# An attention and mixing kernel on one Trainium2 core: the first batches' attention issued younger pair first, with conversions, transfers, and strided work moved around it

## The chip, the cores and the metric

The kernel runs on one core of one Trainium2 chip. The engines are PE (matrix products), DVE (vector work), ACT (activations and copies), POOL (GpSimd), and SP, which here issues most DMAs. The metric is device time in microseconds of one execution. Each engine works through its own instructions in order; an instruction waits for those on other engines whose results it needs.

## The reference

Eight batches, eight heads, 576 positions, 64 elements per head. Heads 0 to 3 attend to a window of 32 positions, heads 4 to 7 to the earlier positions of the same class modulo 32. The result x (576 x 512 for each batch) goes through a low-rank mixing along the sequence (rank 32) and a two-layer network.

```
scores = scale * np.matmul(q, k.transpose(0, 1, 3, 2))
mask_local = (rel >= 0) & (rel < stride)
mask_strided = (rel >= 0) & (pos[None, :] % stride == pos[:, None] % stride)
...
attn = np.exp(scores)
attn = attn / (np.sum(attn, axis=-1, keepdims=True) + 1e-09)
return np.matmul(attn, v).astype(np.float32)
...
h = xt @ U @ V
u = x + h.transpose(0, 2, 1)
ch = np.maximum(u @ w_ch1, 0.0) @ w_ch2
return (u + ch).astype(np.float32)
```

The inner width of the network is 2048.

## The kernel before

**Precision.** fp32 products are made of three products of split operands: high by high, low by high, high by low (uh, ul for u; gh, gl for relu's output; two parts for each weight). U, V and the weights arrive as 64-bit words and are converted on the chip by `to_f32`: L127 on ACT, L129 and L130 on DVE; for a weight L203 (ACT) then makes the high part and L204 (DVE) the low part. U's and V's copies and parts are L142 to L154.

**Units of weights.** A unit is half or all of one of 16 slices fc of the inner width: w0a is the W1 half of fc 0, w0b its W2 half; from fc 7 on one unit holds both. `load_weights` issues their DMAs ahead of time, some held by a 1x1 copy on POOL (L167), a gate; `weights` converts them.

**The first attention.** Batches 0 and 1 go through `first_attention`. A pair is two heads; the eight pairs in `heads` are batch 0's pairs 2, 3, 0, 1 and then batch 1's (numbered 0 to 7 here). Each is a generator: load of q and k, load of v, scores (masks by L338, products by L344), softmax (maximum L354 and subtraction L355 on DVE, exponential L359 on ACT), transposition (L366 on PE, copy L369 on ACT), outputs (L379), normalisation (L388 to L395 on DVE). For batch 0 a fourth step `quarter` follows: transposition of x (L310), its product with U (L284, L286), copies tst (L289, L290 on ACT, L291 on DVE), the product with V (L293) onto the transposed x, and uh (L298, ACT) and ul (L299, DVE). A loop over ticks steps all pairs that are under way, oldest first. `small_weights` loads and converts U and V between. PSUM has two tiles `acc` and one `px` of two banks each; `psx2` hands them out in turn in this part (two of three times acc).

**The main loop.** For each group of 512 tokens and each fc: `gemm1` (12 products, L649), relu to gh (L653, ACT) and gl (L654, DVE), and, one step behind, `gemm2` (12 products, L666). Two slots belong to each fc; at each slot `advance` steps the next batch's attention and mixing (`mix_t` L511 to L526, `mix_u` L534 and L536, `mix_tail` L543 to L549, `transposes` L620, `split`), and `strided_upto` the strided heads of batches 2 to 7: one transfer st, then POOL's products tmp (L440) and DVE's sums of them (L442), later L468 and L470. S0 and S1 give the slots at which it begins and ends; batch 2's first transfer is held by a copy on POOL (L425) that reads a converted weight.

**What sets the order.** A scheduler orders what is emitted by a timeline that it simulates; `issue_after(x)` makes it put an instruction behind x, with no semaphore. `marks` holds instructions for that: "less" the subtractions, "exp", "PT" the copies L369, "norm".

Of the kernel before, what the change touches and what calls it, by code (L numbers as in the profile page):

```python
# [17 lines left out]
NSP = 2  # L18
# [11 lines left out]
S0 = {2: 20, **{b: 32 * (b - 1) - 12 for b in range(3, 8)}}  # L30
S1 = (14, 14)
ORDER0 = (2, 3, 0, 1)
WARM = {0: (320,) * 3, 1: (320,) * 9 + (32,) * 6}
# [4 lines left out]
def fused_kernel(ctx, tc, pairs, strided, U, V, w_in, masks, eye, out):  # L38
# [74 lines left out]
    mask_s = early[:, 1600:1760].bitcast(BF16)  # L113
    raws, w_parts = {}, {}
# [19 lines left out]
    def small_weights():  # L134
# [5 lines left out]
        with tc.issue_after(marks["PT"][0]):  # L140
            f = to_f32(words_in, early, 128, 10 * R)
        nc.scalar.copy(out=U_sb.rearrange("p t r -> p (t r)"), in_=f[:, 0:5 * R])  # L142
        nc.scalar.copy(out=late[0][:, 1816:1816 + 5 * R], in_=f[:, 5 * R:10 * R])
        with tc.issue_after(marks["PT"][0]):
            f = to_f32(words_in[0:R, 10 * R:10 * R + S], att([128, 640], "cu"), R, S)
# [3 lines left out]
        yield  # L149
# [36 lines left out]
    def weights():  # L186
        for i, (fc, x) in enumerate(units):
# [3 lines left out]
            if i < N_HALF:  # L191
                behind = marks["less"][min(7, i + 2)], marks["PT"][min(7, i + 1)]
# [78 lines left out]
    def quarter(pr):  # L271
# [26 lines left out]
        nc.scalar.copy(out=hi, in_=src)  # L298
        nc.vector.tensor_tensor(out=lo, in0=src, in1=hi.bitcast(F32), op=ALU.subtract)  # L299
# [30 lines left out]
    def scores(kT, qT, mask):  # L330
# [3 lines left out]
        with tc.issue_after(done[-1]) if len(done) == 1 else nullcontext():  # L334
            for n in WARM.get(len(done), ()):
                nc.tensor.matmul(sp[:, 0, 0:n], ident_b, mask[:, 0:n], start=True, stop=True, skip_group_check=True)
# [83 lines left out]
    def strided_heads(b):  # L420
# [3 lines left out]
        if b == NSP:  # L424
            nc.gpsimd.tensor_copy(out=st[0:1, 0:1], in_=word_of[units.index((11, None))])  # L425
# [75 lines left out]
    def mix_t(b, half):  # L501
# [8 lines left out]
        for j in range(4):  # L510
            nc.tensor.matmul(ps_a[32 * j:32 * j + 32, :], U_sb[:, j, :], xg[:, j, cs], start=True, stop=False,  # L511
                             skip_group_check=True, tile_position=(0, 32 * j))
# [54 lines left out]
    def first_attention():  # L567
# [6 lines left out]
        dma(out=mask_s, in_=masks[:, 448:768])  # L574
        dma(out=masks_sb, in_=masks[:, 0:448])
        for k, pair in enumerate(heads[0:4]):
            next(pair)
            next(pair)
            if k == 0:
                dma(out=ident, in_=eye)  # L580
            if k == 1:
                next(sw)
        load_ahead(2)
        for tick in range(len(heads) + 3):
            for k in range(len(heads)):
# [5 lines left out]
            if tick in (1, 2):  # L591
                next(sw)
# [65 lines left out]
    def gemm2(n, fc, gh, gl):  # L658
        if fc == 0:
            accs[n] = [ps_acc.tile([128, 2, 512], F32, name="acc") for _ in range(2)]  # L660
        for s in range(4):
# [3 lines left out]
            for i, (gt, part) in enumerate(((gh, 0), (gh, 1), (gl, 0))):  # L665
                nc.tensor.matmul(accs[n][s // 2][:, s % 2, :], gt[:, cs], w_parts[fc, 1][:, part, :],  # L666
                                 start=(fc == 0 and i == 0 and n > 0), stop=(fc == NFC - 1 and i == 2))
# [25 lines left out]
    def strided_upto(slot):  # L693

        nonlocal sgen, sb, sdone, s0, s1
        if sb < B and sgen is None and slot >= S0[sb]:
            sgen, sdone, s0 = strided_heads(sb), 0, slot
# [129 lines left out]
```

## Time and profile before

| | |
|---|---|
| median of 3 runs | 929.31 us (928.73 to 929.73) |
| profiled execution | 927.69 us, span 925.9 us |
| mean granted clock | 0.993 |
| PE | busy 901.9 us (97% of the span) |
| DVE | busy 549.7 us (59%) |
| ACT | busy 243.2 us (26%) |
| POOL | busy 335.5 us (36%) |

The busy times are of the whole span. PE is busy nearly throughout, and the parts where it isn't lie in the first 140 us and the last 126. The rows that follow in the text come from the views of the trace by stretches, by waits, in order of time, by groups of one shape, and from the page's list of DMA issues.

### The profile page before, as it was taken

The page shows a single profiled execution, that of the slowest core. Times are in us where ns is not written, and L with a number is a line of the kernel's source. Part 1 is how long each engine was busy: PE and PEld are TensorE (multiplying, and loading weights), DVE is VectorE, ACT ScalarE, POOL GpSimd, SP SyncE. Part 2 cuts the span into 40 slices and gives each one's busy share as a digit, 9 for nine tenths or more (in the row PEclk, how much of TensorE's full clock was granted, in tenths as well). Part 3 has the DMA queues.
Part 4 walks back from the last instruction along what each step waited for, and adds up shares of the span by engine and source line. Part 5 has one row for each costly group of instructions (what it writes and reads, how often), then busy time and mean ns, then how long its engine had stood idle before and what let it go on. Part 6 is the DMA issues. An engine that isn't in the chain of part 4 may idle for free.

```text
span 925.9 us, 16818 instructions
## 1 busy us (share of the span) xinstructions
PE 901.9 (97%) x7000; PEld 719.1 (78%) x7000; DVE 549.7 (59%) x894; ACT 243.2 (26%) x478; POOL 335.5 (36%) x375
## 2 busy tenths in 40 slices
PE   6899989999999999999999999999999999999997
PEld 4667767877887788778877787778877888888885
DVE  4569898765786587658766786667763341122111
ACT  4447522142123312241224121422142111121110
POOL 1222097344744393439443763456540000000000
PEclk9899999999999999999999999999999999999999
DMA  9779223201330124011500141014200230001001
GB/s 343 272 251 382 84 60 101 73 1 52 92 128 2 52 55 178 1 52 33 181 8 16 52 168 50 1 52 148 73 1 1 57 121 16 1 1 46 0 1 46
DMA packets 39340, 75.29 MB, mean 81 GB/s; under 512 B 6464, under 2 KB 23232, under 8 KB 37344
## 3 DMA queue, kind: packets, MB, share of 16 engines
q1 hardware_dynamic: 27744, 67.13, 20.6%
q10 hardware_dynamic: 10560, 4.73, 2.1%
q0 software_dynamic: 960, 2.36, 0.8%
q8 instruction: 55, 0.90, 0.4%
q14 instruction: 21, 0.17, 0.1%
HBM read 54.14 MB, written 11.67 MB: 71 GB/s over the span
## 4 chain that ended last, share of the span: by engine, by line
PE 89%; DVE 3%; DMA 1%; issue 1%; POOL 1%; ACT 0%; SPq 0%; DVEq 0%; ACTq 0%; POOLq 0%
PE ph L649 41%; PE acc L666 41%; PE px L344 1%; PE px L379 1%; PE px L366 1%; PE px L511 1%; DMA st<-in_strided_dram 1%; PE px L534 1%; DVE cv L130 1%; DVE cv L129 0%; DVE s_st L442 0%; POOL tmp L440 0%; DVE w L204 0%; PE px L515 0%; PE px L338 0%
## 5 line engine op out<-in xcount | busy, mean ns | idle before, releaser
L654 DVE SCALAR_TENSOR_TENSOR gl<-ph,gh 128x512 fp32r<-128x512 f32 x144 | 98.8, 687 | 221.2 <-ACT gh L653 220.5
L649 PE MATMUL ph<-uh,w 128*128 128x512 f32 x648 | 214.7, 392 | 0.0
L653 ACT ACTIVATE gh<-ph 128x512 fp32r<-128x512 f32 x144 | 86.0, 598 | 471.3 <-PE ph L649 385.7
L468 POOL TENSOR_TENSOR tmp<-st,s_st 128x448 f32<-128x448 f32 (+7 forms) x162 | 137.9, 882 | 181.0 <-DVE st L470 95.8
L440 POOL TENSOR_TENSOR tmp<-st 128x576 f32<-128x576 f32 (+6 forms) x162 | 173.8, 1114 | 79.3 <-DMA st<-in_strided_dram 69.4
L666 PE MATMUL acc<-w,gh 128*128 128x512 f32 x648 | 196.9, 391 | 0.0
L470 DVE TENSOR_REDUCE st<-tmp 128x64 f32<-128x64 f32 (+8 forms) x162 | 137.6, 880 | 16.0 <-POOL tmp L468 15.0
L649 PEld LDWEIGHTS ph<-uh,w 128*128 128x128 f32 x648 | 121.2, 188 | 26.1
L666 PEld LDWEIGHTS acc<-w,gh 128*128 128x128 f32 x648 | 121.3, 188 | 25.6
L649 PE MATMUL ph<-ul,w 128*128 128x512 f32 x324 | 127.1, 392 | 0.0
L666 PE MATMUL acc<-w,gl 128*128 128x512 f32 x324 | 121.6, 391 | 3.7 <-DVE gl L654 3.7
L442 DVE TENSOR_REDUCE s_st<-tmp 128x9 f32<-128x576 f32 (+6 forms) x162 | 86.9, 562 | 20.0 <-POOL tmp L440 19.1
L666 PEld LDWEIGHTS acc<-w,gl 128*128 128x128 f32 x324 | 60.8, 188 | 18.0 <-DVE gl L654 4.9
L649 PEld LDWEIGHTS ph<-ul,w 128*128 128x128 f32 x324 | 60.8, 188 | 12.9
L485 ACT COPY xg<-st 32x256 f32<-32x256 f32 x96 | 38.8, 404 | 8.0 <-DVE st L470 6.6
L522 DVE TENSOR_TENSOR ta<-px,ta 32x256 f32<-32x256 f32 x42 | 17.6, 420 | 36.7 <-ACT ta L520 35.7
L672 DVE TENSOR_TENSOR xg<-acc,xg 128x512 f32<-128x512 f32 x36 | 23.0, 681 | 10.2 <-PE acc L666 10.2
L536 DVE TENSOR_TENSOR xg<-px,xg 128x512 f32<-128x512 f32 x28 | 18.0, 686 | 13.1 <-PE px L534 13.1
L649 PE MATMUL ph<-uh,w6a 128*128 128x512 f32 x72 | 25.5, 401 | 0.0
L649 PE MATMUL ph<-uh,w0a 128*128 128x512 f32 x72 | 23.9, 393 | 0.0
L649 PE MATMUL ph<-uh,w1a 128*128 128x512 f32 x72 | 23.8, 389 | 0.0
L666 PE MATMUL acc<-w1b,gh 128*128 128x512 f32 x72 | 23.8, 400 | 0.0
(261 smaller groups left out, 1249.3 us busy)
## 6 DMA issues: line engine op xcount, KB each, us to landing
w<-in_w_dram SPq DMA_DIRECT2D x9, 1024.0 KB, 8.5
out_dram<-xg SPq DMA_DIRECT2D x32, 256.0 KB, 2.1
v<-in_pairs_dram SPq DMA_DIRECT2D x12, 585.0 KB, 5.1
st<-in_strided_dram SPq DMA_DIRECT2D x6, 1152.0 KB, 5.6
qk<-in_pairs_dram SPq DMA_DIRECT2D x12, 576.0 KB, 5.4
late<-in_pairs_dram SPq DMA_DIRECT2D x8, 585.0 KB, 8.8
late<-in_pairs_dram SPq DMA_DIRECT2D x8, 576.0 KB, 9.8
raw<-bt SPq DMA_DIRECT2D x128, 32.0 KB, 1.9
```

The lines of the kernel that those rows point to most:

```text
L440: nc.gpsimd.tensor_tensor(out=tmp[:, 0:n], in0=sk[:, j0:j0 + n], in1=sq[:, i:i + 1].broadcast_to([128, n, D]), op=ALU.mult)
L442: late.append(lambda tmp=tmp, n=n, i=i, j0=j0: nc.vector.tensor_reduce(out=s_st[:, i, j0:j0 + n], in_=tmp[:, 0:n], axis=AX.X, op=ALU.add))
L468: nc.gpsimd.tensor_tensor(out=tv, in0=sv[:, 0:i + 1, d0:d0 + step], in1=s_st[:, i, 0:i + 1].broadcast_to([128, i + 1, step]), op=ALU.mult)
L470: late.append(lambda tv=tv, i=i, d0=d0, step=step: nc.vector.tensor_reduce(out=o_st[:, i, d0:d0 + step], in_=tv.rearrange("p j d -> p d j" ...
L485: nc.scalar.copy(out=xg[32 * i4:32 * i4 + 32, :, cs], in_=o_st[rows, i4:16:4, :])
L522: nc.vector.tensor_tensor(out=ta, in0=ps_a[32 * j:32 * j + 32, :], in1=ta, op=ALU.add)
L536: nc.vector.tensor_tensor(out=xg[:, t + s, :], in0=pv[:, s, :], in1=xg[:, t + s, :], op=ALU.add)
L649: nc.tensor.matmul(ph, w_parts[fc, 0][:, part, 128 * dc:128 * dc + 128], ut[:, dc, :], start=(dc == dcs[0] and i == 0), stop=(dc == dcs[-1 ...
L653: marks.setdefault("gh", []).append(nc.scalar.activation(out=gh, in_=ph, func=AF.Relu).ins)
L654: low = nc.vector.scalar_tensor_tensor(out=gl, in0=ph, scalar=0.0, in1=gh.bitcast(F32), op0=ALU.max, op1=ALU.subtract)
L666: nc.tensor.matmul(accs[n][s // 2][:, s % 2, :], gt[:, cs], w_parts[fc, 1][:, part, :], start=(fc == 0 and i == 0 and n > 0), stop=(fc == ...
L672: nc.vector.tensor_tensor(out=ot, in0=accs[n][s // 2][:, s % 2, :], in1=ot, op=ALU.add)
```

## The change

- The warm-up products ahead of the first two scores (L336, on the masks) become eight and eight of 128x512 on zeros, which DVE writes first into `raw`.
- The masks and the identity are loaded through POOL's queue; on SP the loads of the pairs follow one another in another order, and U and V come behind five of them.
- In a tick the first four pairs are stepped 3, 2, 1, 0.
- U's conversion is held behind the third pair's subtraction, V's also behind the second exponential; V's by-class copies come with a later step. The first four weight units are held behind normalisations and quarters (a new mark, "split") in place of subtractions and copies.
- `mix_t` of batch 1 is held behind the third and fourth `gemm2` (a new mark, "acc").
- Batch 2's strided work: gate on unit 10 in place of 11, its transfer issued at slot 16 in place of 20, and the steps behind it spread from slot 22 to the same end.

```diff
-S0 = {2: 20, **{b: 32 * (b - 1) - 12 for b in range(3, 8)}}
+S0 = {2: 16, **{b: 32 * (b - 1) - 12 for b in range(3, 8)}}
-WARM = {0: (320,) * 3, 1: (320,) * 9 + (32,) * 6}
+WARM = {0: 8, 1: 8}
...
+    zeros = raw.rearrange("p s a d x -> p (s a d x)")[:, 0:320].bitcast(BF16)
+    nc.vector.memset(zeros, 0.0)
...
-        with tc.issue_after(marks["PT"][0]):
+        with tc.issue_after(marks["PT"][0]), tc.issue_after(marks["less"][2]):
             f = to_f32(words_in, early, 128, 10 * R)
...
-        with tc.issue_after(marks["PT"][0]):
+        yield
+        with tc.issue_after(marks["exp"][1]), tc.issue_after(marks["less"][2]):
             f = to_f32(words_in[0:R, 10 * R:10 * R + S], att([128, 640], "cu"), R, S)
...
-                behind = marks["less"][min(7, i + 2)], marks["PT"][min(7, i + 1)]
+                behind = (marks["norm"][2], marks["PT"][3]) if i == 0 else marks["split"][(0, 0, 2, 3)[i]] if i < 4 else \
+                    (marks["less"][min(7, i + 2)], marks["PT"][min(7, i + 1)])
...
-            for n in WARM.get(len(done), ()):
-                nc.tensor.matmul(sp[:, 0, 0:n], ident_b, mask[:, 0:n], start=True, stop=True, skip_group_check=True)
+            for n in range(WARM.get(len(done), 0)):
+                nc.tensor.matmul(sp[:, 0, :], zeros[:, 0:128], zeros[:, 128:640], start=True, stop=True, skip_group_check=True)
...
-            nc.gpsimd.tensor_copy(out=st[0:1, 0:1], in_=word_of[units.index((11, None))])
+            nc.gpsimd.tensor_copy(out=st[0:1, 0:1], in_=word_of[units.index((10, None))])
...
+        with tc.issue_after(marks["acc"][2 + half]) if b < NSP else nullcontext():
+            for j in range(4):
+                nc.tensor.matmul(ps_a[32 * j:32 * j + 32, :], U_sb[:, j, :], xg[:, j, cs], start=True, stop=False,
...
-        dma(out=mask_s, in_=masks[:, 448:768])
-        dma(out=masks_sb, in_=masks[:, 0:448])
-        for k, pair in enumerate(heads[0:4]):
-            next(pair)
-            next(pair)
-            if k == 0:
-                dma(out=ident, in_=eye)
-            if k == 1:
-                next(sw)
+        far_dma(out=mask_s, in_=masks[:, 448:768])
+        far_dma(out=masks_sb, in_=masks[:, 0:448])
+        far_dma(out=ident, in_=eye)
+        for first in (heads[0], heads[1], heads[0], heads[2], heads[1], sw, heads[3], heads[2], heads[3]):
+            next(first)
...
-            for k in range(len(heads)):
+            for k in (3, 2, 1, 0, 4, 5, 6, 7):
...
-            if tick in (1, 2):
+            if tick == 2:
+                next(sw)
                 next(sw)
...
-            sgen, sdone, s0 = strided_heads(sb), 0, slot
+            sgen, sdone, s0 = strided_heads(sb), 0, slot + 6 * (sb == NSP)
+            next(sgen)
...
-        want = N_STRIDED * (slot + 1 - s0) // max(1, s1 - s0)
+        want = (N_STRIDED - 1) * (slot + 1 - s0) // max(1, s1 - s0)
```

Three places show how the order of instructions moves. A row gives the line, the operation, what it writes and reads, and the tile's size; lines of the changed kernel stand some 2 to 5 further down (L359 becomes L363, L127 becomes L129).

ACT from its first exponential on, before: L127 are the first steps of U's and V's conversion, L142 to L147 their copies.

```order
L359 ACTIVATE late<-late 128x640
L369 COPY late<-acc 128x576
L127 ACTIVATE early<-xg 128x320
L127 ACTIVATE late<-xg 32x576
L142 COPY U_sb<-early 128x160
L143 COPY late<-early 128x160
L359 ACTIVATE late<-late 128x640
L146 CAST Vst<-late 32x576
L147 CAST Vst<-late 32x576
L369 COPY late<-acc 128x576
```

After:

```order
L363 ACTIVATE late<-late 128x640
L373 COPY late<-px 128x576
L129 ACTIVATE early<-xg 128x320
L363 ACTIVATE late<-late 128x640
L129 ACTIVATE late<-xg 32x576
L373 COPY late<-acc 128x576
L363 ACTIVATE late<-late 128x640
L144 COPY U_sb<-early 128x160
L145 COPY late<-early 128x160
L149 CAST Vst<-late 32x576
L150 CAST Vst<-late 32x576
```

The second exponential stood behind both conversions and U's copies; it now stands between U's first step and V's, and the third stands ahead of all copies of U and V.

DVE's first instructions, before: L354 and L355 are a pair's maximum and subtraction, L129 and L130 the steps of U (early) and V (late).

```order
L354 TENSOR_REDUCE mx<-acc 128x10
L355 TENSOR_TENSOR late<-acc,mx 128x2x5x64
L129 TENSOR_SCALAR early<-early 128x320
L354 TENSOR_REDUCE mx<-px 128x10
L130 SCALAR_TENSOR_TENSOR early<-xg,early 128x320
L129 TENSOR_SCALAR late<-late 32x576
L355 TENSOR_TENSOR late<-px,mx 128x2x5x64
L130 SCALAR_TENSOR_TENSOR late<-xg,late 32x576
L388 TENSOR_SCALAR rt<-acc 128x10
```

After:

```order
L358 TENSOR_REDUCE mx<-acc 128x10
L359 TENSOR_TENSOR late<-acc,mx 128x2x5x64
L358 TENSOR_REDUCE mx<-acc 128x10
L359 TENSOR_TENSOR late<-acc,mx 128x2x5x64
L358 TENSOR_REDUCE mx<-acc 128x10
L359 TENSOR_TENSOR late<-acc,mx 128x2x5x64
L131 TENSOR_SCALAR early<-early 128x320
L131 TENSOR_SCALAR late<-late 32x576
L132 SCALAR_TENSOR_TENSOR early<-xg,early 128x320
L132 SCALAR_TENSOR_TENSOR late<-xg,late 32x576
```

The maxima and subtractions of the second and third pair now stand ahead of all steps of U and V.

DVE around the eighth and ninth gl of the first group (L654), before: cv and w_ rows are conversions of units 11 to 13 (w_1454 is unit 11, w_1498 and w_1491 are 12, w_1535 is 13), L442 are batch 2's sums.

```order
L654 SCALAR_TENSOR_TENSOR gl<-ph,gh 128x512
L129 TENSOR_SCALAR cv<-cv 128x1024
L130 SCALAR_TENSOR_TENSOR cv<-w_1491,cv 128x1024
L204 TENSOR_TENSOR w_1454<-cv,w_1454 128x2x512
L536 TENSOR_TENSOR xg<-px,xg 128x512 x2
L204 TENSOR_TENSOR w_1498<-cv,w_1498 128x2x512
L654 SCALAR_TENSOR_TENSOR gl<-ph,gh 128x512
L129 TENSOR_SCALAR cv<-cv 128x1024
L442 TENSOR_REDUCE s_st<-tmp 128x1
L442 TENSOR_REDUCE s_st<-tmp 128x2
L130 SCALAR_TENSOR_TENSOR cv<-w_1535,cv 128x1024
```

After (gl is L656, the sums are L446, w_1453 is unit 11, w_1493 unit 12):

```order
L207 TENSOR_TENSOR w_1453<-cv,w_1453 128x2x512
L656 SCALAR_TENSOR_TENSOR gl<-ph,gh 128x512
L446 TENSOR_REDUCE s_st<-tmp 128x1
L446 TENSOR_REDUCE s_st<-tmp 128x2
L131 TENSOR_SCALAR cv<-cv 128x1024
L531 TENSOR_TENSOR tst<-ta,tst 32x256
L446 TENSOR_REDUCE s_st<-tmp 128x3
L446 TENSOR_REDUCE s_st<-tmp 128x4
L132 SCALAR_TENSOR_TENSOR cv<-w_1493,cv 128x1024
```

The first sums stood behind the ninth gl and unit 13's first step; they now stand right behind the eighth gl, ahead of unit 12's first step.

More of the change, by code (lines that the diff above doesn't have):

```diff
@@ L148, in small_weights @@
         nc.vector.tensor_tensor(out=Vst[64:96], in0=f, in1=Vst[0:32].bitcast(F32), op=ALU.subtract)
-        yield
         by_class = Vst.bitcast(F32).rearrange("p (j c) -> p c j", j=NCH)
@@ L297, in quarter @@
         hi, lo = (u[:, pr, :].rearrange("p (j c) -> p j c", c=32) if by_class else u[:, pr, :] for u in (uh, ul))
-        nc.scalar.copy(out=hi, in_=src)
-        nc.vector.tensor_tensor(out=lo, in0=src, in1=hi.bitcast(F32), op=ALU.subtract)
+        one = nc.scalar.copy(out=hi, in_=src)
+        two = nc.vector.tensor_tensor(out=lo, in0=src, in1=hi.bitcast(F32), op=ALU.subtract)
+        marks.setdefault("split", []).append((two.ins, one.ins))
     parts = {}
@@ L509, in mix_t @@
         tst = tsts[b]
-        for j in range(4):
-            nc.tensor.matmul(ps_a[32 * j:32 * j + 32, :], U_sb[:, j, :], xg[:, j, cs], start=True, stop=False,
-                             skip_group_check=True, tile_position=(0, 32 * j))
+        with tc.issue_after(marks["acc"][2 + half]) if b < NSP else nullcontext():
+            for j in range(4):
+                nc.tensor.matmul(ps_a[32 * j:32 * j + 32, :], U_sb[:, j, :], xg[:, j, cs], start=True, stop=False,
+                                 skip_group_check=True, tile_position=(0, 32 * j))
         for j in range(4):
@@ L665, in gemm2 @@
             for i, (gt, part) in enumerate(((gh, 0), (gh, 1), (gl, 0))):
-                nc.tensor.matmul(accs[n][s // 2][:, s % 2, :], gt[:, cs], w_parts[fc, 1][:, part, :],
-                                 start=(fc == 0 and i == 0 and n > 0), stop=(fc == NFC - 1 and i == 2))
+                last = nc.tensor.matmul(accs[n][s // 2][:, s % 2, :], gt[:, cs], w_parts[fc, 1][:, part, :],
+                                        start=(fc == 0 and i == 0 and n > 0), stop=(fc == NFC - 1 and i == 2))
+        marks.setdefault("acc", []).append(last.ins)
     def finish(n):
```

## The prediction

> **What bounds the kernel now.** I read the busy times by stretches of the span first. The columns are: span of the stretch, then busy us (and instructions) of PE, PEld, DVE, ACT, POOL, then the granted clock, DMA share and GB/s.
>
> ```profile
> 18.69:22.10 3.41, 3.41 (x33) 2.86 (x33) 2.61 (x4) 3.17 (x8) 1.49 (x2) 0.50 1.02 410
> 130.00:140.00 10.00, 7.94 (x35) 5.80 (x34) 9.97 (x13) 3.09 (x4) 8.99 (x6) 1.00 0.35 108
> 140.00:800.00 660.00, 660.00 (x4761) 527.91 (x4760) 423.52 (x690) 162.15 (x347) 290.58 (x311) 1.00 0.19 62
> ```
>
> From 140 to 800 us PE is busy in all 660.00 us, so nothing there can be won or lost except by a new stop. PE does the same products after the change. So the time moves only by what PE waits, or runs at half clock, ahead of 140 us. PE's waits are the second view (total us, times, longest):
>
> ```profile
> PE acc L666 <- DVE gl L654: 3.7, 3, 1.9
> PE acc L379 <- issue: 2.0, 1, 2.0
> PE px L511 <- DVE xg L391: 1.6, 1, 1.6
> ```
>
> Two groups matter: the prefix (all rows but the first), and gl, the low half of relu's output, which DVE makes between the first strided reductions of batch 2 near 125 us. I argue against the profiled execution, 927.69 us with a span of 925.9; the median of the runs shown is 929.31, so I carry a difference over to the median.
>
> **The prefix.** PE's timeline (start, us, engine, line, operation, wait in brackets) has these marks. L310 is each quarter's transposition of x, L284 its product with U, L649 the first product with W1, L366 the transpositions of a pair (here pair 5).
>
> ```profile
> 19.15 2.69 PE L310 MATMUL acc<-ident,early 128*128 128x128 f32 x10
> 36.39 1.13 PE L310 MATMUL px<-ident,xg 128*128 128x128 f32 x8
> 37.45 1.06 PE L284 MATMUL ph<-xg,U_sb 128*32 128x128 f32 x8
> 42.43 1.88 PE L310 MATMUL acc<-ident,xg 128*128 128x128 f32 x8 [0.42 <-DVE xt L395]
> 44.24 1.92 PE L284 MATMUL ph<-xg,U_sb 128*32 128x128 f32 x8
> 49.10 0.50 PE L649 MATMUL ph<-uh,w0a 128*128 128x512 f32 x1
> 52.97 0.86 PE L366 MATMUL px<-ident,late 128*128 128x128 f32 x5
> ```
>
> Before, pair 1's softmax stands on DVE behind U's conversion, which waits for ACT, which waits for U's transfer; its reduction L354 runs only at 14.43. Rows of ACT and DVE:
>
> ```profile
> 12.31 0.64 ACT L369 COPY late<-acc 128x576 f32<-128x576 f32 x1 [2.54 <-PE acc L366]
> 13.66 0.50 ACT L127 ACTIVATE early<-xg 128x320 f32<-128x320 f32 x1 [0.71 <-DMA xg<-in_U_dram]
> 14.40 0.71 ACT L127 ACTIVATE late<-xg 32x576 f32<-32x576 f32 x1 [0.24 <-DMA xg<-in_V_dram]
> 16.77 0.74 ACT L359 ACTIVATE late<-late 128x640 f32<-128x640 f32 x1 [0.54 <-DVE late L355]
> 17.44 0.67 ACT L146 CAST Vst<-late 32x576 fp32r<-32x576 f32 x1
> 14.43 0.82 DVE L354 TENSOR_REDUCE mx<-px 128x10 f32<-128x640 f32 x1
> 18.63 0.75 DVE L148 TENSOR_TENSOR Vst<-late,Vst 32x576 fp32r<-32x576 f32 x1
> ```
>
> Rows of the DMA issues (KB each, median us from issue to landing; od is the scratch in DRAM that POOL's queue writes):
>
> ```profile
> late<-in_pairs_dram SPq DMA_DIRECT2D x8, 576.0 KB, 9.8
> od<-early POOLq DMA_DIRECT2D x2, 256.0 KB, 6.7
> masks_sb<-in_masks_dram SPq DMA_DIRECT2D x1, 112.0 KB, 2.1
> ```
>
> After, DVE's reductions of pairs 1 and 2 stand ahead of U's, so that block is gone on DVE. On ACT, though, U's first instruction now stands ahead of pair 1's exponential: the exponential still waits for U's transfer. That transfer is issued some 0.9 us earlier (two masks and the identity no longer stand ahead of it on SP, one other does) but pair 2's q and k, 576 KB, now go ahead of it: at the 410 GB/s of the row of 18.69 to 22.10 us that is 1.4 us, so U, usable at 13.66 before, is usable at some 14.2, and I take 14.4. My chain, an estimate from these durations: conversion of U 14.4 to 14.9, exponential to 15.65 (before it began at 16.77); V 0.71 and pair 1's copy 0.64 to 17.2 with small gaps; exponential of pair 2 0.74 to 17.9; two copies of U, near 0.3 each, and two of V, 0.67 each, to 19.9; L148's 0.75 to 20.6; pair 3's reduction and subtraction, 0.82 each, to 22.3. Only then is its PSUM bank free for the first quarter: 22.3, which is 3.2 **later** than the 19.15 of before. From there the younger-first order pays: pairs 2 and 3 have their scores and exponentials done already, so nothing stands between the quarters but outputs, normalisation, and copies. By the same durations the second quarter comes at 28.4, the third at 36.1 (before 36.39), the fourth at 41.8, and W1's first product at 44.0 against 49.10. PE does other work between than before, so I compare the end of pair 5's transpositions: 52.97 + 0.86 = 53.83 before, 47.5 after, 6.3 earlier. From 49.10 to 52.97 PE did 14 products of W1 and the start of pair 6's scores; of these 3.87 us only seven products, some 1.7, stand ahead after, so 2.2 us of work is merely left for later: **the gain is 6.3 - 2.2 = 4.1 us**. It rests on this chain with no new stops; each microsecond that U lands later takes one away.
>
> Costed at nothing: the 16 warm-up products on zeros, whose cover is PE's wait for the first pair's transfer (if that cover were gone, 8 products at 0.50 us at most as in the L649 row, 4 us, once); the masks and the identity moved to POOL's queue, whose cover is the time from 12 to 15 us in which PE waits for U anyway (a POOL transfer beside SP's full queue took 6.7 us, the masks on SP 2.1, so 4.6 later at worst; what goes past 3 us counts one for one); the 0.1 us memset. The hold on mix_t moves L511 behind the products of w4a, but the second half of those products needs the bank that the same normalisation frees: the 1.64 us stop moves to another row, worth 0. The 2.0 us stop in L379 ("issue") has no releaser in the trace, so I keep it (between 0 and -2.0).
>
> **The clock** is the term with a sign of its own.
>
> ```profile
> 39.17:42.58 3.41, 1.98 (x54) 1.34 (x44) 2.54 (x8) 2.10 (x5) 0.39 (x4) 1.00 0.69 213
> 42.58:46.00 3.42, 3.42 (x16) 2.67 (x16) 0.30 (x1) 0.67 (x2) 0.00 (x0) 0.50 1.03 327
> ```
>
> Behind a stretch of 3.41 us with PE busy for 1.98, the next 3.42 us ran at half clock; the fourth quarter's 1.88 + 1.92 stand beside the third's 1.13 + 1.06, so such a stretch costs 1.6 us where PE is the path. After the change PE pauses at 12 to 15.6 and again at 33.6 to 36.1. The first pause is followed by work that waits for ACT and DVE, so half clock there hides; behind the second one, it delays the third quarter and W1's start. Whether the 2.5 us fall into one stretch depends on its phase: I take half, **+0.8** (between 0 and +3.2).
>
> The Trainium skill ("TensorE: Matmul & The Clock Gate", "Part 1: The HAM clock gate (the "warmup" mystery)") speaks of a free-running activity window of about 3.4 us, so that what a pause costs depends on where the window falls; the steps above, 3.41 and 3.42 us, agree. By that rule both new pauses could halve the clock, and the sum would be +0.7 instead of -1.7: this is rival B, priced from the rows alone.
>
> **The strided stage.** Batch 2's strided work (POOL multiplies, DVE reduces) starts behind a gate and a 1.15 MB transfer:
>
> ```profile
> 99.75 1.05 ACT L203 CAST w<-cv 128x1024 fp32r<-128x1024 f32 x1
> 107.31 1.08 POOL L425 COPY st<-w 1x1 f32<-1x1 f32 x1 [19.04 <-ACT w L203]
> 115.39 11.74 POOL L440 TENSOR_TENSOR tmp<-st 128x64 f32<-128x64 f32 x11 [7.00 <-DMA st<-in_strided_dram]
> st<-in_strided_dram SPq DMA_DIRECT2D x6, 1152.0 KB, 5.6
> 115.74 0.22 DVE L442 TENSOR_REDUCE s_st<-tmp 128x1 f32<-128x64 f32 x1 [2.72 <-POOL tmp L440]
> L129 DVE TENSOR_SCALAR cv<-cv 128x1024 int32<-128x1024 int32 x6 | 4.1, 682 | 0.3 <-ACT cv L127 0.3
> L130 DVE SCALAR_TENSOR_TENSOR cv<-w,cv 128x1024 int32<-128x1024 int32 x6 | 7.3, 1218 | 0.1
> L204 DVE TENSOR_TENSOR w<-cv,w 128x1024 fp32r<-128x1024 f32 x6 | 7.3, 1216 | 0.0
> L442 DVE TENSOR_REDUCE s_st<-tmp 128x9 f32<-128x576 f32 x11 | 8.1, 740 | 2.1 <-POOL tmp L440 2.1
> L129 DVE TENSOR_SCALAR cv<-cv 128x1024 int32<-128x1024 int32 x2 | 2.4, 1221 | 0.0
> L130 DVE SCALAR_TENSOR_TENSOR cv<-w,cv 128x1024 int32<-128x1024 int32 x3 | 5.3, 1781 | 0.0
> L204 DVE TENSOR_TENSOR w<-cv,w 128x1024 fp32r<-128x1024 f32 x3 | 4.7, 1574 | 0.0
> 125.19 1.76 DVE L129 TENSOR_SCALAR cv<-cv 128x1024 int32<-128x1024 int32 x1
> 129.75 2.19 DVE L130 SCALAR_TENSOR_TENSOR cv<-w,cv 128x1024 int32<-128x1024 int32 x1
> 141.72 1.83 DVE L204 TENSOR_TENSOR w<-cv,w 128x1024 fp32r<-128x1024 f32 x1
> ```
>
> The three grouped rows with x6 are of 60 to 112 us (POOL mostly idle), the next four of 115 to 152 us (POOL busy): conversions take 0.54, 0.56 and 0.36 us more beside POOL. After the change the gate stands behind w10's conversion, one unit earlier, and the first reductions stand behind the eighth gl instead of behind the ninth and w13's first step. The 99.75 row is w10's: the gate's copy then ends at 101.9, and the transfer, 5.6 us from issue by its median, lands near 107.6 in the frame of before (108.8 at the 6.8 us of this execution). The eighth gl ends near 106, so DVE waits about 1.9 us there instead of 2.72: -0.8. Up to gl of fc 12, four more conversion steps run beside POOL (2 x 0.54 + 0.56 + 0.36 = +2.0) and three more reductions stand ahead (3 x 0.74 at most, one is shorter: +2.0); w15's last step, 1.57, moves behind: 2.0 + 2.0 - 1.6 - 0.8 = **+1.6** on top of the gl stops, 3.7 us, which stay. Bounds: -3.5 where the earlier start spreads the work and the stops go; +6.6 where the landing takes 6.8 us and each of the twelve steps its longest row (4 x (1.76 + 2.19 + 1.83) = 23.1 against 18.3 by the means: 4.8 more, and 0.2 net for the landing).
>
> The Trainium skill ("SBUF — State Buffer", "Who interferes with whom") has a rule that speaks against this part: a vector instruction with two SBUF inputs, or in a two-port mode, takes a port pair shared with GpSimd, and whoever comes second blocks entirely. The steps with x2 and x3 above, longer beside POOL, agree; by a full block each would wait for one whole POOL multiplication, and the sum would be that of rival C, +3.3 instead of -1.7.
>
> **Sum.** -4.1 + 0.8 + 1.6 = -1.7: 926.0 for the profiled execution, and 927.6 for the median.
>
> **Rivals.**
> A, the stops go as well: the earlier transfer spreads the strided work and the gl stops vanish (-3.5), the clock stays full. -4.1 - 3.5 = -7.6, 921.7; with the 2.0 us stop gone too, 919.7. For it: DVE waits 2.72 us for the first product of POOL. Against it: DVE is 9.97 of 10 us busy at 130 us, and the change adds work to just that stretch.
> B, the prefix's gain is eaten: half clock in two stretches on the path, +3.2 in place of +0.8, or U landing 2.5 us later, or the masks late by as much. -4.1 + 3.2 + 1.6 = +0.7, 930.0. That the change doesn't do what it says belongs here: the exponentials are still bound by U's transfer, through ACT's order in place of DVE's.
> C, slower: the conversions of w12 to w15 all run beside POOL, with reductions put ahead of them, and gl of fc 11 and 12 comes later than PE can wait. At the longest rows -4.1 + 0.8 + 6.6 = +3.3, 932.6. It decides for slower from a cost of 5.2 us in this stage on. For it: DVE's 9.97 busy; against it: the longest rows would have to be the rule.
>
> **How the numbers follow.** Forecast 0.42 (its own range 925 to 930), A 0.24, B 0.18, C 0.16. 0.2%, 1.9 us, is about what a measurement of this kernel can tell from no change: faster lies under 927.4, slower over 931.2. The forecast gives 0.22 faster and 0.20 same (it lies at the bound, with the unfixed 2.0 us stop on the fast side), A 0.24 faster, B 0.14 same and 0.04 slower, C 0.15 slower and 0.01 same: 0.46, 0.35, 0.19. The range takes in most of A and C: 920.5 to 932.0, with 2 in 10 outside.
>
> **What would show it.** In the profile after: the first exponential behind U's conversion at 14.9 to 15.7 (later means U); the first quarter at 22.3, W1's first product at 44, pair 5's transpositions at 47.5; half clock between 36 and 40 or not; a stop of some 1.6 us at the second half of the products of w0b, still released by the normalisation; the first L446 near 107 less the prefix's gain, and gl stops of about 5.3 us in all. The prediction is wrong if pair 5 is reached less than 3 us earlier, if the strided transfer lands late, or if a stop turns up after 150 us.

## The result, and the profile after

The changed kernel takes 934.54 us in the median of four runs (934.40 to 934.82) against 929.24 of the kernel before: a ratio of 1.0053, with a 95% interval of 1.0038 to 1.0068. It is **slower by 5 us**, where 927.6 was forecast and 932.0 was the upper end of the range. The profiled execution took 934.82 us, with a span of 932.6 (925.9 before).

PE's timeline of the changed kernel, with start, duration, line, and the wait ahead in brackets. L342 are the mask products ahead of the first scores, L348 scores, L383 outputs, L314 the first quarter's transposition, L651 the first product with W1, L370 at 55.87 pair 5's and at 71.41 pair 7's transpositions.

```profile
8.11 0.44 PE L342 MATMUL acc<-early,masks_sb 128*128 128x320 bf16 x2 [3.26 <-DMA masks_sb<-in_masks_dram]
18.68 0.37 PE L348 MATMUL acc<-late 64*32 64x32 f32 x20
22.38 1.06 PE L348 MATMUL acc<-late 64*32 64x64 f32 x52 [3.33 <-issue]
24.71 1.21 PE L383 MATMUL px<-late 64*32 64x65 f32 x70
28.82 0.35 PE L383 MATMUL px<-late 64*32 64x65 f32 x10 [2.91 <-issue]
29.10 2.69 PE L314 MATMUL acc<-ident,early 128*128 128x128 f32 x10
52.55 0.50 PE L651 MATMUL ph<-uh,w0a 128*128 128x512 f32 x1
55.87 0.86 PE L370 MATMUL px<-ident,late 128*128 128x128 f32 x5
71.41 0.80 PE L370 MATMUL px<-ident,late 128*128 128x128 f32 x5
80.62 0.47 PE L666 MATMUL acc<-tst,Vst 96*128 96x512 f32 x1 [1.94 <-DVE xt L399]
143.15 0.80 PE L668 MATMUL acc<-w,gl 128*128 128x512 f32 x1 [3.56 <-DVE gl L656]
```

Two stops stand in the middle of a run of equal products (20 of pair 3's 72 scores done; 70 of pair 1's 80 outputs done) and have no releaser. The first quarter comes at 29.10, where 22.3 was predicted, and W1's first product at 52.55 instead of 44.0. Pair 5's transpositions, by which the prediction was to be judged, end at 56.73, where 47.5 was predicted and 53.83 stood before. Pair 7's transpositions, which both kernels reach with nearly the same work done, stand at 71.41, against 67.41 before: the prefix lost 4.0 us. The busy times up to that point (length, then PE, PEld, DVE, ACT, POOL, granted clock, DMA share, GB/s), for the kernel before and the changed one:

```profile
0.00:67.41 67.41, 54.93 (x1328) 40.54 (x1329) 38.77 (x73) 28.52 (x52) 12.21 (x31) 0.92 0.80 290
```

```profile
0.00:71.41 71.41, 57.67 (x1326) 40.16 (x1328) 38.35 (x74) 27.93 (x52) 14.26 (x34) 0.88 0.78 274
```

PE's idle time grew from 12.48 to 13.74 us, by 1.3, its busy time by 2.7. The warm-up products, before and after, are most of the latter:

```profile
3.40 0.98 PE L336 MATMUL acc<-early,masks_sb 128*128 128x320 bf16 x3 [3.40 <-DMA masks_sb<-in_masks_dram]
7.21 2.74 PE L336 MATMUL px<-early,masks_sb 128*128 128x320 bf16 x15
```

```profile
1.26 3.60 PE L340 MATMUL acc<-raw 128*128 128x512 bf16 x8 [1.26 <-DVE raw L115]
10.13 2.57 PE L340 MATMUL acc<-raw 128*128 128x512 bf16 x7 [0.33 <-issue]
```

They took 3.72 us and now take 6.17. Without them PE is busy for 51.2 and 51.5 us, nearly the same, though the clock is 0.88 instead of 0.92. Against the kernel before, nearly all of the 4.0 us is thus time in which PE waits or only warms up (16.2 us before, 19.9 after). The warm-up products themselves show no cost: the run without them, warm0 below, is no faster. And behind 100 us the strided stage adds its part. The waits and the stretches at half clock in the changed kernel:

```profile
PE acc L668 <- DVE gl L656: 5.1, 3, 3.6
PE acc L348 <- issue: 3.8, 2, 3.3
PE px L383 <- issue: 2.9, 1, 2.9
```

```profile
29.00:39.24 10.24, 10.24 (x123) 7.74 (x114) 2.76 (x9) 2.86 (x6) 2.21 (x4) 0.50 0.68 223
141.38:144.80 3.42, 1.65 (x4) 1.37 (x5) 3.42 (x4) 0.13 (x1) 2.10 (x2) 0.54 0.29 117
144.80:148.20 3.40, 3.40 (x9) 2.63 (x9) 3.34 (x6) 0.92 (x1) 2.67 (x2) 0.50 0.00 1
```

Behind the stop of 2.91 us the quarters run at half clock for 10.24 us; in and behind the gl stop of 3.56 us the main loop does so for nearly 7, of which 5.3 lie behind the stop. Before there was no half clock between 46 us and the tail. The products of the main loop, compared one by one, stand 2.8 us later than before at 120 us and 6.65 later from 170 us on: 2.8 from the prefix (of its 4.0 us at pair 7, 1.2 are made up again on the way), 3.9 from the strided stage, together the 6.7 by which the span grew.

### The profile page after: what moved, and what is told of

Read it like the earlier page. It is cut to its first block, busy times and chain, and to the rows that moved or that the text cites. A ratio compares the mean times of both kernels' runs of the same rounds, so it can differ in the third digit from the quotient of the medians.

```text
span 932.6 us, 16816 instructions
## 1 busy us (share of the span) xinstructions
PE 905.5 (97%) x6997; PEld 719.9 (77%) x6998; DVE 550.1 (59%) x895; ACT 243.2 (26%) x478; POOL 337.3 (36%) x378
## 4 chain that ended last, share of the span: by engine, by line
PE 86%; DVE 3%; POOL 1%; DMA 1%; issue 0%; ACT 0%; DVEq 0%; POOLq 0%
PE acc L668 41%; PE ph L651 40%; PE px L383 1%; PE px L348 1%; PE px L370 1%; PE px L516 1%; DVE s_st L446 1%; PE px L539 1%; DMA st<-in_strided_dram 1%; DVE w L207 1%; POOL tmp L444 1%; DVE cv L132 0%; DVE cv L131 0%; PE px L342 0%; PE px L520 0%
## 5 line engine op out<-in xcount | busy, mean ns | idle before, releaser
L656 DVE SCALAR_TENSOR_TENSOR gl<-ph,gh 128x512 fp32r<-128x512 f32 x144 | 99.0, 688 | 231.0 <-ACT gh L655 230.2
L651 PE MATMUL ph<-uh,w 128*128 128x512 f32 x648 | 215.7, 394 | 0.0
L651 PEld LDWEIGHTS ph<-uh,w 128*128 128x128 f32 x648 | 121.7, 188 | 26.8
L651 PE MATMUL ph<-ul,w 128*128 128x512 f32 x324 | 126.6, 391 | 0.0
L446 DVE TENSOR_REDUCE s_st<-tmp 128x9 f32<-128x576 f32 (+6 forms) x162 | 87.2, 563 | 18.6 <-POOL tmp L444 17.6
L668 PEld LDWEIGHTS acc<-w,gl 128*128 128x128 f32 x324 | 61.4, 189 | 19.7 <-DVE gl L656 6.3
L651 PEld LDWEIGHTS ph<-ul,w 128*128 128x128 f32 x324 | 61.1, 189 | 12.5
L643 DVE TENSOR_TENSOR ul<-raw,uh 128x512 fp32r<-128x512 f32 x32 | 21.4, 695 | 5.0 <-ACT uh L642 5.0
L651 PE MATMUL ph<-uh,w6a 128*128 128x512 f32 x72 | 24.3, 398 | 0.0
L651 PE MATMUL ph<-uh,w0a 128*128 128x512 f32 x72 | 24.0, 391 | 0.0
L651 PE MATMUL ph<-uh,w5a 128*128 128x512 f32 x72 | 23.8, 391 | 0.0
```

The source lines that it names most:

```text
L446: late.append(lambda tmp=tmp, n=n, i=i, j0=j0: nc.vector.tensor_reduce(out=s_st[:, i, j0:j0 + n], in_=tmp[:, 0:n], axis=AX.X, op=ALU.add))
L643: nc.vector.tensor_tensor(out=lo, in0=raw[:, :, :, dc, :], in1=hi.bitcast(F32), op=ALU.subtract)
L651: nc.tensor.matmul(ph, w_parts[fc, 0][:, part, 128 * dc:128 * dc + 128], ut[:, dc, :], start=(dc == dcs[0] and i == 0), stop=(dc == dcs[-1 ...
L656: low = nc.vector.scalar_tensor_tensor(out=gl, in0=ph, scalar=0.0, in1=gh.bitcast(F32), op0=ALU.max, op1=ALU.subtract)
L668: last = nc.tensor.matmul(accs[n][s // 2][:, s % 2, :], gt[:, cs], w_parts[fc, 1][:, part, :], start=(fc == 0 and i == 0 and n > 0), stop= ...
```

## The experiments

All twelve change one or a few parts. Each was compared with the kernel before on one chip, but for warm0 and light, which ran once. There single runs of the kernel before spread from 926.5 to 933.5, and one profiled execution may lie 2 to 3 us beside its median (best1: 927.01 against 929.82); the ratios are the measure, and the profiles show where the time is in one execution. Half clock is the time below full clock in the first 80 us, and from 80 to 200 us, added up from the trace's steps of 3.41 us.

| kernel | median, us | ratio to before (95%) | span | half clock, us |
|---|---|---|---|---|
| before | 929.24 | | 925.9 | 10.2, 0 |
| changed | 934.54 | 1.0053 (1.0038 to 1.0068) | 932.6 | 17.1, 6.8 |
| u_strided | 932.86 | 1.0046 (1.0028 to 1.0064) | 929.9 | 13.7, 6.8 |
| b_strided | 932.46 | 1.0047 (1.0026 to 1.0068) | 930.1 | 13.7, 3.4 |
| u_masks | 934.41 | 1.0055 (1.0035 to 1.0074) | 932.3 | 23.9, 6.8 |
| u_order | 931.51 | 1.0031 (1.0013 to 1.0048) | 928.5 | 3.4, 3.4 |
| warm0 | 934.97 (one run) | | 932.9 | 23.9, 6.8 |
| light | 935.98 (one run) | | 934.2 | 17.1, 6.8 |
| best1 | 929.82 | 0.9993 (0.9972 to 1.0014) | 925.0 | 6.8, 3.4 |
| b_order | 931.11 | 1.0014 (0.9994 to 1.0035) | 930.2 | 23.9, 0 |
| gate11 | 934.21 | 1.0072 (1.0046 to 1.0098) | 931.3 | 13.7, 6.8 |
| best3 | 924.11 | 0.9940 (0.9918 to 0.9962) | 922.0 | 13.7, 0 |
| young3 | 930.9 | 1.0014 (1.0000 to 1.0029) | 928.8 | 21.4, 5.9 |
| old3 (best3 again) | 923.83 | 0.9937 (0.9918 to 0.9957) | 922.2 | 17.1, 0 |

**The theory of the blocks.** In the changed kernel I counted PE's instructions (products and weight loads) ahead of the stops, from the busy times by stretch:

```profile
0.00:16.00 16.00, 10.81 (x222) 5.40 (x223) 3.62 (x5) 3.38 (x5) 2.02 (x7) 0.89 0.90 331
16.00:19.10 3.10, 2.96 (x127) 2.06 (x128) 2.50 (x5) 2.23 (x4) 0.02 (x1) 1.00 1.02 413
19.10:26.00 6.90, 3.54 (x127) 2.75 (x127) 4.32 (x8) 3.08 (x6) 2.17 (x4) 0.75 1.02 410
```

445, then 255, then 254: 445, 700 and 954 instructions up to the stops. The trace also holds PE's semaphore and drain instructions, which these views leave out: 3, 4 and 6 of them ahead of the three stops. With them the stops of 0.42 us at 16.08, 3.33 at 22.38 and 2.91 at 28.82 stand at 448, 704 and 960 from the start, 256 apart. A fourth one, 1.02 us at 61.27, and the one stop without releaser in the kernel before, 1.97 us at 57.27, stand at 2240, which is 448 and seven times 256. Counted in this way, every stop of over 0.5 us without a releaser that any of the kernels here has in its first 65 us stands within two instructions of 448, 704, 960, 1216, or 2240. In the list of queues, a queue of kind "instruction" moves one block of 0.02 MB in each case: this is it, in the stretch from 19.7 to 20.0 us of the changed kernel,

```profile
q8 instruction: 1, 0.02, 22.5%
```

and the next one in 26.2 to 26.5. So the theory: PE gets its program in blocks of 256 instructions, and a block's transfer stands in line with the data. The first transfers began at 13.73, 19.84 and 26.30 us in the changed kernel and at 11.04, 17.25, 23.77 and 29.95 in the kernel before: one in 6.1 to 6.5 us, while 384 to 412 GB/s moved from 10 to 30 us in both. PE went on some 2.5 us after the start of a transfer that it waited for. So while the transfer engines are that full, PE gets 256 instructions in somewhat over 6 us in either kernel, and a pair's scores, transpositions and outputs alone are 159 products, 318 instructions. What asks for a block is not shown: from PE's entry into a block to the next one's transfer passed 3.8 us at 16.08 in the changed kernel, but 0.1 at 23.63 in the kernel before, with as much data moving. The Trainium skill ("Runtime: NRT & Kernel Launch", "Instruction fetch mechanics") says the same of the unit, 16 KiB or 256 instructions, refilled by a DMA queue; it calls the cost mostly hidden, and there the runs differ: 6.2 us in two stops here.

*warm0*: no warm-up products.

```diff
-WARM = {0: 8, 1: 8}
+WARM = {0: 0, 1: 0}
-    nc.vector.memset(zeros, 0.0)
```

> The changed kernel without its 16 warm-up products (32 PE instructions with their weight loads) and without the zeros. Theory, PE stops where its next block of 256 instructions has not arrived: the stops stay at the same count of instructions from the start (448, 704, 960), so in the program 16 products later: the stop in pair 3's scores stands behind about 36 of its 72 products instead of 20, and the one in pair 1's outputs (70 of 80) moves into quarter 0's transpositions (about 6 of 10). Rival, the stops wait for data or a bank: they stay behind 20 and 70 products.

PE's timeline of it (L347 scores, L313 the first quarter's transpositions):

```profile
20.19 0.77 PE L347 MATMUL acc<-late 64*32 64x32 f32 x36
22.72 0.85 PE L347 MATMUL acc<-late 64*32 64x64 f32 x36 [1.76 <-issue]
26.07 0.94 PE L313 MATMUL acc<-ident,early 128*128 128x128 f32 x6
29.35 1.20 PE L313 MATMUL acc<-ident,early 128*128 128x128 f32 x4 [2.35 <-issue]
```

The stops moved 16 products on, to 36 of 72 and to 6 of 10, exactly where the count puts them, and into other lines. They wait for neither data nor a bank. The time didn't move (934.97 against 934.82 in the profiled executions).

*light*: the first four weight loads, 2 MB, held until pair 3's exponential.

```diff
-        if k > 1:
-            for i in (2 * k - 2, 2 * k - 1):
+        if k > 2:
+            for i in range(0 if k == 3 else 2 * k - 2, 2 * k):
...
-        load_ahead(2)
```

> The changed kernel with the loads of w0a, w1a, w2a and w3a (2 MB) held behind pair 3's exponential, so that the transfer engines have less to do between 16 and 27 us. Theory, the next block's transfer stands in line behind data: the stop at instruction 960 falls from 2.9 to under 1.2 us, the one at 704 from 3.3 by 0 to 2. Rival, the delay is fixed by PE's own pace: both stay within 0.4 us. The weights come later, so the total time says little.

PE's waits of this kernel up to 30 us, and its stretches around the second block; then the same stretches of the changed kernel:

```profile
PE acc L348 <- issue: 3.1, 1, 3.1
PE px L383 <- issue: 1.2, 1, 1.2
```

```profile
22.00:25.00 3.00, 2.91 (x127) 2.30 (x127) 1.65 (x2) 1.15 (x2) 0.70 (x2) 0.70 0.75 219
25.00:28.00 3.00, 1.81 (x19) 1.53 (x16) 1.12 (x3) 1.48 (x5) 0.77 (x6) 0.50 0.54 151
```

```profile
22.00:25.00 3.00, 2.62 (x81) 2.00 (x88) 1.49 (x2) 0.18 (x1) 0.71 (x2) 0.53 1.01 410
25.00:28.00 3.00, 0.92 (x70) 0.75 (x53) 0.16 (x1) 2.44 (x6) 0.29 (x2) 0.90 1.03 403
```

Up to 22 us the queues are full in both, and the stop at 704 stays (3.1). Behind it they moved 219 and 151 GB/s instead of 410 and 403, the next block's transfer began 4.5 us after the one ahead instead of 6.5, and the stop at 960 fell from 2.9 to 1.2, at the edge of what was expected. The wait for the block follows the load on the transfer engines. (The weights come later, and the whole is slower.)

**Which parts cost.** *u_order*: the old order of the ticks.

```diff
-            for k in (3, 2, 1, 0, 4, 5, 6, 7):
+            for k in range(len(heads)):
```

> The changed kernel with the ticks' oldest-first order put back (masks still on POOL's queue, conversions held). Theory: PE reaches its instruction blocks later than they arrive, so no stop without releaser over 1.2 us before 50 us, and the first W1 product at 50 us or earlier instead of 52.55; time minus 2 to minus 4, 930.5 to 932.5. Rival, the order is good and only masks and U hold the prefix: plus 0 to plus 4.

The sum came as expected in the profile (928.5, 4.1 less) and in the ratio (1.0031 against 1.0053, though their intervals overlap), the mechanism did not: stops of 2.1, 2.0 and 1.2 us without releaser are still there (and W1's first product comes at 50.10, just past the 50 expected). The stretch up to pair 7's transpositions, and that of best1 (below), whose program is the same as far as this:

```profile
0.00:66.16 66.16, 52.54 (x1325) 36.65 (x1327) 38.41 (x74) 28.14 (x52) 12.92 (x31) 1.00 0.84 295
```

```profile
0.00:66.29 66.29, 56.35 (x1325) 38.87 (x1327) 38.23 (x74) 28.29 (x52) 12.87 (x31) 0.95 0.84 295
```

u_order is idle for 13.62 us, as much as the changed kernel's 13.74, but busy for 52.54 instead of 57.67, at a full clock instead of 0.88. That looks as if the order cost through the clock alone. best1 speaks against it: it was at half clock for 6.8 us, busy for 56.35 and idle for 9.94 only, and it came to the same place. The three kernels that share the changed one's prefix (changed, u_strided, gate11) reach pair 7 at 71.41, 70.13 and 70.80, the two that share u_order's at 66.16 and 66.29: that the order costs 4 to 5 us up to there is repeated, but how they divide into stops and half clock is not settled.

One thing the traces do show. Up to instruction 960 both orders keep the same pace: they enter the block at 704 at 22.4 us in both, the one at 960 at 28.8 and 28.4 (28.0 in the kernel before). From 16 to 28 us PE runs the same number of instructions in the changed kernel (first row) and in u_order (second), but it is busy for 6.50 us in the one and for 8.30 in the other:

```profile
16.00:28.00 12.00, 6.50 (x254) 4.81 (x255) 6.83 (x12) 6.74 (x14) 2.48 (x6) 0.86 1.02 409
16.00:28.00 12.00, 8.30 (x255) 6.02 (x254) 6.76 (x14) 7.05 (x15) 3.52 (x6) 1.00 1.03 411
```

The orders differ in what fills these blocks. In u_order the first quarter with its long products lies among them, from 18.63 us on; in the changed kernel they hold scores, transpositions and outputs, most of them short, and the quarters come behind, at half clock. So the blocks limit what the order can gain, whichever it is.

*b_order*: the younger-first order alone, in the kernel before.

```diff
-            for k in range(len(heads)):
+            for k in (3, 2, 1, 0, 4, 5, 6, 7):
```

> The kernel before with the younger-first order alone. The predicted step: the prefix ends 4.1 us earlier, 925. Theory of the instruction blocks: PE meets blocks that have not arrived, stops of over 2 us behind 700 to 960 instructions and half clock behind them, and the prefix ends 0 to 4 us later than before: 929 to 933.

Pair 7's transpositions stand at 72.32 (67.41 before), with 23.9 us at half clock; the span is 930.2. Over all runs the ratio is 1.0014, with 1 inside its interval: no gain, and a loss only by the profiled execution. A gain of 4.1 us from the order alone is excluded: it would be a ratio near 0.9956, and the interval ends at 0.9994. (The prediction had the held conversions with it; young3 below has both.)

*u_masks*: the masks and the identity on SP's queue, as before.

```diff
-        far_dma(out=mask_s, in_=masks[:, 448:768])
-        far_dma(out=masks_sb, in_=masks[:, 0:448])
-        far_dma(out=ident, in_=eye)
+        dma(out=mask_s, in_=masks[:, 448:768])
+        dma(out=masks_sb, in_=masks[:, 0:448])
...
+            if n == 2:
+                dma(out=ident, in_=eye)
```

> The changed kernel with the masks and the identity back on SP's queue, ahead of the pairs' loads as before. First scores at 5.5 to 6.0 instead of 8.49. Theory: PE's stops without a releaser are arrivals of its next block of 256 instructions, which set the pace from the second pair on; they stay (about 3 us each at instructions 704 and 960), and the time falls by 0 to 2.5 us, 932 to 934.5. Rival, the masks' late landing is what the prefix lost: minus 4 or more, 930.5 or less.

The time is that of the changed kernel (934.41), at the upper edge of what was expected. PE starts earlier (first scores at 5.48) and then stops three times for its blocks (2.3, 2.3, and 1.0 us, the first two less than the 3 expected) and once, 3.0 us, for an exponential: it enters the block at 448 at 12.4 instead of 16.1, but the one at 704 at 21.9 instead of 22.4. Here the masks' late landing is hidden behind the pace of the blocks. *u_strided*: the strided part put back.

```diff
-S0 = {2: 16, **{b: 32 * (b - 1) - 12 for b in range(3, 8)}}
+S0 = {2: 20, **{b: 32 * (b - 1) - 12 for b in range(3, 8)}}
-            nc.gpsimd.tensor_copy(out=st[0:1, 0:1], in_=word_of[units.index((10, None))])
+            nc.gpsimd.tensor_copy(out=st[0:1, 0:1], in_=word_of[units.index((11, None))])
-            sgen, sdone, s0 = strided_heads(sb), 0, slot + 6 * (sb == NSP)
-            next(sgen)
+            sgen, sdone, s0 = strided_heads(sb), 0, slot
-        want = (N_STRIDED - 1) * (slot + 1 - s0) // max(1, s1 - s0)
+        want = N_STRIDED * (slot + 1 - s0) // max(1, s1 - s0)
```

> The changed kernel with the strided part alone put back (first transfer at slot 20, gate on unit 11, old spreading). Theory: the early strided work costs 3.5 to 4.6 us by itself (a 3.6 us gl stop near 140 us and a half-clock stretch of 6.8 us behind it), so 930 to 931, with no gl stop over 2.2 us and no half clock after 50 us. Rival, the lateness of gl comes from the prefix, which leaves DVE behind with its conversions: the time stays within 1 us of 934.5 and the stop stays.

The span falls by 2.7, the median by 1.7, the ratio to the kernel before by 0.0007 only, which is inside the intervals; the main loop's products, 0.3 us late at 120 us against the changed kernel, are 3.0 early from 170 us on, and the longest gl stop is 2.2. A half-clock stretch is left behind it, against the expectation, and another one, worth 1.6 us, has come behind the stop at 80 us, so the sum is short of what was expected. *b_strided* is the reverse of that diff in the kernel before.

> The kernel before with the strided part of the change alone. Theory: plus 3 to 5 us, 932 to 934, with a gl stop of about 3.5 us near 138 us. Rival, only the changed prefix makes it late: 929 within 1 us. Second rival, the predicted one: the earlier start spreads the work, 925 to 927.

932.46, a ratio of 1.0047. Its waits and the stretch behind its longest stop:

```profile
PE acc L666 <- DVE gl L654: 4.9, 3, 3.6
137.10:140.50 3.40, 3.40 (x10) 2.63 (x9) 3.34 (x5) 0.00 (x0) 3.40 (x3) 0.53 0.24 87
```

Without any of the changed prefix, the strided part makes the 3.6 us stop and the half clock behind it. Its products are 1.7 us late ahead of the stage, in this execution, and 4.5 from 170 us on: 2.7 us in this stage.

*gate11*: only the gate of the first strided transfer.

```diff
-            nc.gpsimd.tensor_copy(out=st[0:1, 0:1], in_=word_of[units.index((10, None))])
+            nc.gpsimd.tensor_copy(out=st[0:1, 0:1], in_=word_of[units.index((11, None))])
```

> The changed kernel with the gate of batch 2's first transfer alone put back on unit 11 (slots and spreading as changed). Theory, the one unit is what puts the sums ahead of unit 12's first step and all conversions beside POOL: the longest gl stop falls from 3.6 to under 2.3 us, no half clock behind 130 us, and the span falls by 2.5 to 4 us (929 to 930). Rival, the slots make it: within 1 us of 932.6.

```profile
PE acc L668 <- DVE gl L656: 2.6, 2, 2.2
```

The gate brings the longest gl stop from 3.6 to 2.2 us, as much as the whole strided part put back, and the main loop's products from 1.0 us late against the changed kernel, at 120 us, to 2.3 early at 200: the one unit makes the stop as long as it is. But half clock from 134.8 to 138.2 is still there, against the expectation, one more stretch of it fell behind the stop at 80 us, and 0.8 is given back near 230 us, from a cause that is open. The median (934.21, a ratio of 1.0072) shows no gain, so that the gate's share of the time is shown by one profiled execution only.

**Putting both back.** *best1* is u_order and u_strided together.

> The changed kernel with both the strided part and the oldest-first order put back; masks on POOL's queue, zeros, held conversions and mix stay. Theory, these two parts are what costs: 0 to 1.5 us faster than the kernel before (927.5 to 929.3), PE clock full from 11 us to 75 us. Rival, the losses of the two don't add (one hides the other): 931 or more.

929.82, a ratio of 0.9993: no difference from the kernel before, with 0.9 us less span and a median 0.5 above the expected range. The loss of 5 us is gone with these two parts. That the clock would be full wasn't so (6.8 us at half). *best3* has the masks on SP's queue as well (the diff of u_masks on top), and *old3* is the same kernel again.

> The changed kernel with the strided part and the order put back and the masks and the identity on SP's queue as well; zeros, held conversions, held mix and the new order of loads stay. With the younger-first order the masks' queue made no difference, since the instruction blocks set the pace. If that pace binds here too: the same as with the masks on POOL's queue, a span of 925 within 0.5. If PE's start is what binds with the older order: 1.5 to 2.5 us less, 922.5 to 923.5, a version faster than both kernels.

> The fastest version again, beside the run with the younger-first order on the same chip: 922.5 to 925.5, faster than the kernel before by 0.4 to 0.8%, and the clock at half for less than 15 us of the first 80.

924.11 and 923.83 (spans of 922.0 and 922.2): ratios of 0.9940 and 0.9937, **faster than both kernels by over 5 us**. So what is left of the change (zeros as warm-up, the order of the loads, held conversions, held mix) gains, once the two parts and the masks' queue are back; which of the four gains was not separated. The time is near the one expected if PE's start binds, but the profiles don't show that cause. best3's first scores run at 5.71 instead of best1's 8.56, yet it reaches pair 7 at 66.90 (old3 at 68.81, best1 at 66.29), and at 120 us its main loop is 1.3 us behind best1's. It gets ahead, by 2.7, between there and 170 us, with a longest gl stop of 0.9 instead of 2.2 and no half clock. Why that stop is shorter is open. old3 had half clock for 17.1 us of the first 80, more than the 15 expected, and was as fast. *young3* is best3 with the younger-first order.

> The version that was fastest so far (strided part put back, masks and identity on SP's queue) with the younger-first order of the change. Theory: the order alone costs through blocks that have not arrived (two stops over 2 us between 12 and 30 us) and half clock for 10 us or more behind them; 3 to 6 us slower than the same with the older order, 927 to 930. The predicted step would have it faster by up to 4.

930.9 beside 923.83 on the same chip: the order costs 7 us here. The expectation was 3 to 6 slower than the other and 927 to 930, so it is somewhat more. PE's waits, of young3 and of old3:

```profile
PE acc L348 <- issue: 3.8, 2, 2.3
PE px L383 <- issue: 2.3, 1, 2.3
PE acc L669 <- DVE gl L657: 2.2, 1, 2.2
PE acc L667 <- DVE xt L399: 2.0, 1, 2.0
```

```profile
PE acc L669 <- DVE gl L657: 1.5, 2, 0.9
PE acc L383 <- issue: 0.9, 1, 0.9
PE acc L667 <- DVE xt L399: 0.9, 1, 0.9
```

The stops for blocks are 6.1 us against 0.9. Yet the main loop's first products are only 1.4 us later; the rest comes behind: the stop for pair 7's normalisation is 2.0 instead of 0.9 and a half-clock stretch follows it (2.9 us late from 84 us on), and a gl stop of 2.2 instead of 0.9 brings another one (6.6 late from 170 us on). In the main loop one pair of stops of 0.85 us each, 2.3 us apart, had half clock behind it (best3 at 75.2; the same pair in old3 had not). The stops near 2 us had it in some kernels (both of young3) and not in others (1.94 us in the changed kernel), and the 3.6 us ones always.

The costs do not add. By the ratios, each with an interval of some 0.2% to either side, the strided part costs 0.47% in the kernel before and 0.38% under the older order (u_order against best1), but 0.07% in the changed kernel; the masks' queue costs 0.53% between best1 and best3 and nothing in the changed kernel. One loss can cover another, as the blocks cover the masks; for the strided part why is not settled.

## Why the prediction was wrong

**U's transfer and the second exponential.** Predicted: the exponential waits for U and runs at 14.9 to 15.65. ACT's rows of the changed kernel:

```profile
15.18 0.52 ACT L129 ACTIVATE early<-xg 128x320 f32<-128x320 f32 x1
15.58 0.75 ACT L363 ACTIVATE late<-late 128x640 f32<-128x640 f32 x1
18.28 0.74 ACT L363 ACTIVATE late<-late 128x640 f32<-128x640 f32 x1
```

It ran at 15.58, but not for that reason: U's conversion waited for nothing of U; it stood behind pair 0's copy, which was late since the masks landed 6 us after their issue on POOL's queue and the first scores ran at 8.49 instead of 5.97. I had taken 4.6 us later as the worst and 3 us of cover. In this kernel the cover held all the same (u_masks), through a pace that I had not seen. With the other parts put back the masks' queue costs 0.53% (best1 and best3), but not at PE's start, as far as the profiles show.

**The chain to the first quarter: the step that failed.** "By the same durations" I let each step run as soon as its inputs were there, so that PE's order was free to be denser, and I kept the one stop without releaser (2.0 us at 57.27) as a thing of its own place. It was a sign of a limit: 256 instructions at a time, a block in 6.1 to 6.5 us under full queues. My chain had "no new stops"; there PE went through the scores and outputs faster than their instructions came. Stops of 3.33 and 2.91 us took the first quarter from 22.3 to 29.10. In place of the 4.1 us gained, the prefix lost 4.0 at pair 7.

**The clock** was given a term of +0.8, up to +3.2, for a pause at 33.6 to 36.1. The pauses came elsewhere, at 19 to 22.4 and 25.9 to 28.8, the first one was followed by one stretch at half clock (22.2 to 25.6), the second by three, 10.24 us. The mechanism was right, the place was not. What the clock cost against the kernel before is small all the same: that one had 10.2 us at half clock ahead of pair 7 too, and PE's products without the warm-up were busy for 0.3 us more after the change. That the term's size is near this is luck.

**The hold on mix_t**, worth 0: right. The stop of 1.64 us became one of 1.94 at the second half of gemm2's first products, behind the same normalisation.

**The strided stage**: +1.6 in gl stops predicted; 5.1 against 3.7 measured, so +1.4. DVE's conversions and the start of the stage in the changed kernel:

```profile
104.15 1.24 POOL L429 COPY st<-w 1x1 f32<-1x1 f32 x1 [12.67 <-ACT w L206]
111.33 0.22 DVE L446 TENSOR_REDUCE s_st<-tmp 128x1 f32<-128x64 f32 x1 [1.29 <-POOL tmp L444]
L132 DVE SCALAR_TENSOR_TENSOR cv<-w,cv 128x1024 int32<-128x1024 int32 x4 | 7.1, 1764 | 0.0
L207 DVE TENSOR_TENSOR w<-cv,w 128x1024 fp32r<-128x1024 f32 x4 | 6.8, 1707 | 0.0
L131 DVE TENSOR_SCALAR cv<-cv 128x1024 int32<-128x1024 int32 x4 | 5.4, 1356 | 0.0
```

The conversions took 1764, 1707 and 1356 ns beside POOL, near the 1781, 1574 and 1221 that I had used. What the sum lacked is what a stop costs behind itself: nearly 7 us at half clock at 141 to 148 us, in a stage where PE is the path. The stage cost 3.9 in all; less the 1.4, that leaves 2.5 for the 5.3 us of half clock behind the stop. Of the rivals C had the mechanism (conversions beside POOL, sums put ahead, gl of the last units late), at a price built from the longest rows instead of from the clock; the forecast had the size of the stops' growth. Rival B's outcome for the prefix, the gain eaten, was true too and more than true, through stops that it didn't name; and both came at once, which no case had.

## What to carry to other kernels

A stop in the middle of equal instructions that has no releaser may be the next block of the program: count instructions between such stops, semaphore instructions with them, and don't count on a denser order while the transfer queues are full. Price a stop with the half clock that may follow it: a stretch of 3.4 us in the main loop cost 1.4 to 1.6 us more here (best1 against u_order at 75 us; u_strided, gate11 and light against the changed kernel at 80). When parts are undone one at a time and each gives back little, undo them together before calling the rest useless; here the rest was worth 5 us.

## What the runs showed of the hardware

PE's program arrived in blocks of 256 instructions: one in 6.1 to 6.5 us beside 384 to 412 GB/s of data, 4.5 us after the one ahead at about 200 (light, from 19.58 to 24.09), and 2.5 us from a transfer's start until a waiting PE went on. The masks landed 6 us after their issue on POOL's queue beside a full SP queue, against 2.1 as the first transfers on SP's. Of the half clock, which pause starts it and for how many stretches (one to six were seen, 3.4 us each) differed between kernels with nearly the same pauses; what decides the number was not settled.
